# Every engine's instruction order as a table, with each tile's buffer named

## The chip, the cores and the metric

The kernel runs on one core of a Trainium2 chip. The metric is the device time of one execution in microseconds (us). The core has five engines with a queue each, which run side by side and meet at semaphores: PE (matrix multiply; PEld is its loading of weights), DVE and ACT (vector work and activation functions), POOL (a slower vector engine), and SP, which here issues the DMA transfers. An engine runs its own instructions strictly in the order in which the program lists them.

## The reference

Three layers follow each other, on a batch of 4, 576 tokens and 512 features (8 heads of 64):

```python
def attention(q, k, v):                       # (4, 8, 576, 64)
    pooled = repeat(softmax_attn(mean4(q), mean4(k), mean4(v)), 4)   # 144 pooled positions
    local = softmax_attn(q, k, v, mask=abs(i - j) < 4)
    return pooled + local                     # heads side by side: x, (4, 576, 512)

def moe(x):
    u = x + real(fft(fft(x, axis=1), axis=2))
    un = (u - mean(u)) / sqrt(var(u) + 1e-6)
    return u + maximum(un @ w_ch1, 0) @ w_ch2     # 512 -> 2048 -> 512

def moe2(x):
    gate = sigmoid(causal depthwise conv of 5 taps over the tokens)
    return (gate * (x @ w_val)) @ w_out
```

The result is float32. The weights arrive as float64 words.

## The kernel before

**Stages.** Each batch first goes through attention and the Fourier step: scores `dS` of the local band (a mask matmul from `bandb`, then products of kT and X), `exp` on ACT (dP), transposes (dPT, PT), values (dO); the pooled part `qkT`, `sc`, `E`, `eT`, `po`, `base`; then the FFT as matrix products (`ab`, AH and AL, then `pp`, `pq`, with the sum X<-X,DS). After it the batch is three units of 192 tokens, twelve in all. A unit has a layer normalization (`st`, `uc`, `sq`, `vv`, the root `r` by steps on POOL or DVE, and uh and ul, the f16 high and low part), eight h groups (`ph`, line 995) and eight c groups (`pc`, line 1015), each of 24 matmuls, since each product is made of three f16 passes (high x high, high x low, low x high). Between an h group and its c group ACT makes hh from ph and DVE the remainder hl. Then follow the sum X<-pc, and the third layer: yy (X in two f16 parts), the taps of the convolution, `val` (line 1107), gh and gl, `out` (line 1123), osb and its store. Unit (0,0) alone is computed in f32 (lines 957 and 970), because its weights aren't scaled yet.

**Weights.** They are loaded as words, put together on DVE in three integer steps (W<-W, W<-raw), and kept as f32 until a power of two to scale them by is known. For W1 ACT sums the squares (line 380), a PE product `tot` adds them across partitions, ACT makes f2s from it (line 259) and POOL turns it into s_w by p2a, p2b and s_w (lines 246, 248, 250). For W2 it is the product `gram` on PE, whose diagonal `tr<-gram,eye` DVE takes (line 179); gram lies in the bank that `pc` uses next. For w_val ACT squares (`sqw`), PE adds (`po<-sqw,corner`), DVE takes the maximum `cvmx`, and POOL makes s_wv. Then ACT writes the high part (line 406) and DVE the low one (line 176: W<-W,s_w,W).

**What sets the order.** All is written as small functions with a place in the program's order (`put`, `spread`; the P_ and S_ numbers), run in the order of their places. The framework then schedules each instruction by a time model and by priorities: `urgent` (line 184) raises a function's by the number of its kind in the table `U`. Loads are chained to each other (`load`, line 193). `behind` lets single instructions wait for an earlier one of another engine or the same, as the weights' conversion (line 300) for a step of the unit before. Batch 0's attention has a written order of steps, CHAIN0, which `line` holds engine by engine (line 344). Tiles of a ring (`bufs` of 2 or 3) take its buffers as they become free in the scheduled order. The loop at the end runs all of it:

```python
    for _, _, f in sorted(events):
        f()
```

Of the kernel before, what the change touches and what calls it, by code (L numbers as in the profile page):

```python
# [11 lines left out]
BF16 = mybir.dt.bfloat16  # L12
# [24 lines left out]
N_FILL = (8, 5, 14)  # L37
CHAIN0 = """
# [18 lines left out]
CHAIN = True  # L57
S_CH = 1.3
# [22 lines left out]
U = {'D': 4000, 'F': 3000, 'N': 3000, 'X': 600, 'M': 0, 'V': 1000, 'O': 0, 'W': 0, 'R': 2000, 'S': 4000}  # L81
# [55 lines left out]

@with_exitstack
def attn_moe_kernel(ctx, tc, q_t, k_t, v_p, v_w, w1, w2, w_val, conv_t, w_out, c_feat, c_seq, c_band, c_eye, c_plm, out):
# [4 lines left out]
    def pool(name, bufs=1, **kw):  # L144
        return ctx.enter_context(tc.tile_pool(name=name, bufs=bufs, **kw))
# [15 lines left out]
    dram = pool("dram", 2, space=bass.MemoryType.DRAM)  # L161
# [29 lines left out]
    chain = {"on": CHAIN, "last": None, "after": None}  # L191

    def load(**kw):

        if chain["on"] and chain["last"] is not None:
            with tc.issue_after(chain["last"]):
                i = nc.sync.dma_start(**kw)
        elif chain["after"] is not None:
            with tc.issue_after(chain["after"]):
                i = nc.sync.dma_start(**kw)  # L200
        else:
            i = nc.sync.dma_start(**kw)
        chain["last"] = i.ins

# [85 lines left out]
    gates, gates1, gates2 = [], [], []  # L290

    def behind(gate, f):

        if gate is None:
            f()
        else:
            with tc.issue_after(gate):
                f()

    def to_f32(dst, raw, gate=lambda: None):  # L300

        r = raw.rearrange("p (n t) -> p n t", t=2)
        behind(gate(), lambda: V.tensor_scalar(out=dst, in0=r[:, :, 1], scalar1=3, scalar2=0x3FFFFFF8,
                                               op0=ALU.logical_shift_left, op1=ALU.bitwise_and))
        behind(gate(), lambda: stt(V, dst, r[:, :, 1], -0x40000000, dst, ALU.bitwise_and, ALU.bitwise_or))
        last = []
        behind(gate(), lambda: last.append(stt(V, dst, r[:, :, 0], 29, dst, ALU.logical_shift_right, ALU.bitwise_or)))
        return last[0]

    def word_op(dst, raw, k):  # L310
# [5 lines left out]
        elif k == 1:  # L316
            stt(V, dst, r[:, :, 1], -0x40000000, dst, ALU.bitwise_and, ALU.bitwise_or)
        else:
            stt(V, dst, r[:, :, 0], 29, dst, ALU.logical_shift_right, ALU.bitwise_or)

# [21 lines left out]
    lined = {}  # L342

    def line(f):

        n0 = len(nc.cur_bb.bb.instructions)
        f()
        for i in nc.cur_bb.bb.instructions[n0:]:
            if i.engine != nc.sync.engine:
                if i.engine in lined:  # L350
                    tc.add_manual_dep(i, lined[i.engine], mybir.DependencyInfo(
                        mybir.DependencyClass.NoSync, mybir.DependencyReason.DATA), reason="line")
                lined[i.engine] = i.name

    def word_w(i):
        if i < 16:
            raw = raws.pop(i)
            n = 1024 // len(raw)
            pos = AT[i] if i < 8 else 8
            for z, x in enumerate(raw):  # L360
                last = to_f32(W[AT[i] + 1].bitcast(I32)[:, z * n:(z + 1) * n], x,
                       lambda g=gates if pos < 4 else gates1 if pos < 8 else gates2: g.pop(0) if len(g) > 1 else g[0])
            if i == 11:
                st[0]["worded"] = last
# [10 lines left out]
    def sumsq_w(i, key, first, last):  # L375

        if key == "w1":
            if first:
                gram[key] = keep.tile([P, 8], F32, name="ss_" + key)
            behind(st[0]["sq"].ins, lambda: A.activation(  # L380
# [478 lines left out]
    def ln(b, j):  # L859
# [27 lines left out]
        if head:  # L887
            st[0]["sq"] = i
# [825 lines left out]
```

## Time and profile before

| | us |
|---|---|
| median of 3 runs | 712.53 (712.43 to 714.36) |
| profiled execution, its own time | 715.93 |
| its span, first to last instruction | 714.1 |
| PE busy | 668.3 (94%) |
| DVE busy | 465.0 (65%) |
| ACT busy | 323.1 (45%) |
| POOL busy | 129.8 (18%) |
| mean granted clock of PE, as a share of 2.4 GHz | 0.974 |

Busy time is a sum over instructions, and the stages of the program differ: in the first 130 us weights arrive and batch 0 is prepared, then units follow each other, and the attention of the next batch runs between them. From some 520 us on only units are left. A stage is read from a table of windows: its length, the busy time of each engine in it, and the clock that PE was granted. The gap between length and busy time is the time the engine stood.

### The profile page before, as it was taken

What the parts mean: (1) busy time and instruction counts of PE and PEld (TensorE: products, weight loads), DVE (VectorE), ACT (ScalarE), POOL (GpSimd) and SP (SyncE); (2) the same over time, 40 slices, a digit from 0 to 9 for tenths busy, and PEclk for the clock granted to TensorE, in tenths of its full rate; (3) what the DMA queues carried; (4) which work ended last, traced back from release to release, by engine and by line L of the source; (5) the groups of instructions that cost most, each with busy time, mean ns of one, the idle gap of its engine ahead of it and who ended that gap; (6) DMA issues with size and microseconds to landing.
All of it is one profiled execution on the core that took longest, in us unless ns stands there. A gap on an engine that the chain in (4) does not pass through costs nothing. (4 is left out here: it accounts for less than half of the span.)

```text
span 714.1 us, 18255 instructions
## 1 busy us (share of the span) xinstructions
PE 668.3 (94%) x7778; PEld 588.7 (82%) x7779; DVE 465.0 (65%) x962; ACT 323.1 (45%) x985; POOL 129.8 (18%) x178
## 2 busy tenths in 40 slices
PE   7778998899989679999999999999999999999997
PEld 3555897889889568888898798798899989999895
DVE  4979999599884786548778527649435672723324
ACT  3843745693522556666334744744313232222212
POOL 0260042501121513230302324003100110000000
PEclk9968999999999879999999999999999999999999
DMA  9990144302333001330130001002000000000001
GB/s 331 410 339 2 59 178 161 122 31 81 127 113 115 17 1 40 112 104 16 60 110 1 25 25 35 17 35 79 4 17 16 2 17 16 2 17 2 30 2 45
DMA packets 23299, 52.08 MB, mean 73 GB/s; under 512 B 1855, under 2 KB 11071, under 8 KB 22194
## 3 DMA queue, kind: packets, MB, share of 16 engines
q1 hardware_dynamic: 23218, 50.91, 20.0%
q8 instruction: 61, 1.00, 0.6%
q14 instruction: 20, 0.16, 0.1%
HBM read 44.41 MB, written 8.26 MB: 74 GB/s over the span
## 5 line engine op out<-in xcount | busy, mean ns | idle before, releaser
L995 PE MATMUL ph<-uh,W 128*128 128x192 f16 x1408 | 195.4, 246 | 0.0
L995 PEld LDWEIGHTS <-W 128*128 128x128 f16 x2112 | 175.2, 98 | 5.9 <-issue 3.6
L995 PE MATMUL ph<-ul,W 128*128 128x192 f16 x704 | 173.2, 246 | 0.0
L1015 PE MATMUL pc<-hh,W 128*128 128x192 f16 x1232 | 170.8, 246 | 0.4 <-ACT hh L999 0.4
L1015 PEld LDWEIGHTS <-W 128*128 128x128 f16 x1848 | 153.3, 98 | 6.6 <-issue 4.5
L1015 PE MATMUL pc<-hl,W 128*128 128x192 f16 x616 | 150.4, 246 | 0.9 <-DVE hl L176 0.8
L176 DVE SCALAR_TENSOR_TENSOR hl<-ph,hh 128x384 f16<-128x384 f32 x88 | 48.5, 553 | 94.3 <-ACT hh L999 94.2
L999 ACT ACTIVATE hh<-ph 128x384 f16<-128x384 f32 x88 | 43.1, 490 | 101.1 <-PE ph L995 98.0
L1107 PE MATMUL val<-yy,W 128*128 128x192 f16 x576 | 55.7, 254 | 10.0 <-ACT yy L1049 6.6
L176 DVE SCALAR_TENSOR_TENSOR W<-X,cw,W 128x192 f32<-128x192 f32 x160 | 61.0, 435 | 0.7 <-ACT W L1070 0.5
L1107 PEld LDWEIGHTS <-W 128*128 128x128 f16 x576 | 50.5, 101 | 12.7 <-issue 6.5
L1123 PE MATMUL out<-W,gh 128*128 128x512 f16 x144 | 45.8, 379 | 0.0
L561 ACT ACTIVATE dP<-dS,dmx 128x64 f32<-128x64 f32 x120 | 36.0, 333 | 2.3 <-PE dPT L580 2.0
L179 POOL TENSOR_TENSOR E<-E,lsu 72x288 f32<-72x288 f32 x16 | 22.1, 1395 | 43.7 <-DVE lsu L694 22.8
L176 DVE SCALAR_TENSOR_TENSOR W<-W,W 128x1024 int32<-128x1024 int32 x24 | 29.2, 1237 | 0.1
L970 PE MATMUL pc<-h,W 128*128 128x192 f32 x128 | 24.9, 348 | 3.1 <-DVE tr L179 2.2
L1123 PE MATMUL out<-W,gl 128*128 128x512 f16 x72 | 27.3, 379 | 0.0
L561 ACT ACTIVATION_READ_ACCUMULATOR dP<-dS,dmx 128x1 f32 x120 | 27.2, 226 | 0.0
L176 DVE SCALAR_TENSOR_TENSOR X<-pc,iv,X 128x384 f32<-128x384 f32 x22 | 12.9, 613 | 20.0 <-PE pc L1015 20.0
L970 PEld LDWEIGHTS pc<-h,W 128*128 128x128 f32 x128 | 22.3, 202 | 3.8 <-DVE tr L179 2.4
L1123 PEld LDWEIGHTS <-gh 128*128 128x128 f16 x144 | 14.1, 98 | 13.6 <-issue 0.2
L182 POOL TENSOR_TENSOR sq<-sq 128x384 f32<-128x384 f32 (+1 forms) x12 | 11.9, 994 | 72.8 <-ACT sq L886 72.4
(287 smaller groups left out, 1228.6 us busy)
## 6 DMA issues: line engine op xcount, KB each, us to landing
W<-in_moe_w_ch_dram SPq DMA_DIRECT2D x12, 1024.0 KB
out_dram<-osb SPq DMA_DIRECT2D x17, 256.0 KB
vw<-in_vw_dram SPq DMA_DIRECT2D x8, 512.0 KB
X<-in_q_dram SPq DMA_DIRECT2D x6, 576.0 KB
v<-in_vp_dram SPq DMA_DIRECT2D x24, 144.0 KB
kT<-in_k_dram SPq DMA_DIRECT2D x4, 582.0 KB
X<-in_moe_w_ch_dram SPq DMA_DIRECT2D x2, 1024.0 KB
raw<-in_moe_w_ch_dram SPq DMA_DIRECT2D x4, 512.0 KB
```

Of the source, the lines that this page charges most:

```text
L176: return eng.scalar_tensor_tensor(out=out, in0=in0, scalar=scalar, in1=in1, op0=op0, op1=op1)
L179: return eng.tensor_tensor(out=out, in0=a, in1=b, op=ALU.mult)
L182: return eng.tensor_tensor(out=out, in0=a, in1=b, op=ALU.add)
L561: A.activation(out=s_[:, z, a], in_=pss[par][:, z, a], func=AF.Exp, scale=SCALE, bias=mx[:, par, z, a:a + 1], accum_out=su[:, par, z, a:a ...
L970: T.matmul(out=c["ps"][m // 2][:, m % 2], lhsT=W[9 + g][:, o:o + 128], rhs=hs[g // 2][:, g % 2, e, :], start=(kk == 0 and m % 2 == 0), sto ...
L995: T.matmul(out=ps[:, e], lhsT=w1_ap(pw, kc, 2 * g + e), rhs=uh[px][:, kc, :], start=(t == 0), stop=(t == 11))
L999: A.activation(out=h_, in_=ps, func=AF.Relu)
L1015: T.matmul(out=ps[m // 2][:, m % 2], lhsT=w2_ap(pw, kk, m), rhs=x[px][:, e, :], start=(kk == 0 and (pw, px) == (0, 0) and m % 2 == 0), sto ...
L1107: T.matmul(out=ps[:, e], lhsT=wv_ap(pw, kc, 2 * mh + e), rhs=m_["y"][px][:, kc, :], start=(t == 0), stop=(t == 11))
L1123: T.matmul(out=ps, lhsT=(gh, gl)[px][:, kc, t * 128:(t + 1) * 128], rhs=wo_ap(pw, kc), start=(n == 0), stop=(n == 11))
```

## The change

The numbers `U`, the priorities, the chains of loads, the gates `behind` and the helper `line` are gone. Two tables take their place. `ORDER` has one text for each engine, in which every instruction of the program stands once, as event and number within the event ("5.1" is instruction 1 of event 5, "0-3" a run of them). `SLOT` says for each tile of a ring which buffer it takes. Both were searched for offline; neither the search nor its model is in the source. Events are still made by `put` and `spread`, and what each instruction computes is the same. At the end each instruction is tied to the one ahead of it in its engine's text, without a semaphore, so that the scheduler can only list them in that order. PE, DVE, ACT, POOL and SP have the same instructions as before, one by one.

```diff
+SLOT = {
+    "ps_s.s": "010101010101010101010101010101010101010101010101010101010101011010010101010101010101010101010101010101010101010101010101010101010101010101001010101001010101010",
...
+ORDER = {
+    "sync": """
+4 0 1 2 7 3 6 9 11 5.1 5.0 10 8 13 14 15.0 12 15.3 15.1 15.4 198.1 15.5 15.2 125.0 198.0 124.1 16.2 124.0 121.0 16.1
...
-U = {'D': 4000, 'F': 3000, 'N': 3000, 'X': 600, 'M': 0, 'V': 1000, 'O': 0, 'W': 0, 'R': 2000, 'S': 4000}
...
+class Rings:
...
+    def tile(self, shape, dt, name, tag=None, bufs=None):
+        bufs = bufs or self.bufs
+        if tag is None or bufs == 1:
+            return self.pool.tile(shape, dt, name=name, **({"tag": tag} if tag else {}))
+        k = self.n[tag] = self.n.get(tag, -1) + 1
+        z = SLOT.get(f"{self.name}.{tag}")
+        return self.pool.tile(shape, dt, name=name, tag=f"{tag}_{int(z[k]) if z else k % bufs}")
...
-    def urgent(f, key):
-        if U[key]:
-            with tc.high_priority(offset=U[key]):
-                f()
-        else:
-            f()
...
     def load(**kw):
-
-        if chain["on"] and chain["last"] is not None:
-            with tc.issue_after(chain["last"]):
-                i = nc.sync.dma_start(**kw)
...
+        nc.sync.dma_start(**kw)
...
-    def behind(gate, f):
-
-        if gate is None:
-            f()
-        else:
-            with tc.issue_after(gate):
-                f()
...
-    put(S_G1[1], lambda: urgent(w1_scale, "S"))
+    put(S_G1[1], w1_scale)
...
+    engines = {n: getattr(nc, n).engine for n in ORDER}
+
+    def traced(f, n0):
+        f()
+        return [i for i in nc.cur_bb.bb.instructions[n0:] if "Boundary" not in type(i).__name__]
...
+    parts = [traced(lambda: None, 0)]
     for _, _, f in sorted(events):
-        f()
+        parts.append(traced(f, len(nc.cur_bb.bb.instructions)))
+    for name, eng in engines.items():
+        line = []
+        for x in ORDER[name].split():
+            n, _, r = x.partition(".")
+            ins = [i for i in parts[int(n)] if i.engine == eng]
+            z, _, y = r.partition("-")
+            line += ins[int(z):int(y or z) + 1] if r else ins
+        assert len(line) == len(set(i.name for i in line)) == sum(i.engine == eng for p in parts for i in p)
+        for x, y in zip(line, line[1:]):
+            tc.add_manual_dep(y, x.name, mybir.DependencyInfo(
+                mybir.DependencyClass.NoSync, mybir.DependencyReason.DATA), reason="order")
```

Three places of the order follow; the line numbers in rows of the new kernel are its own.

DVE, in the stage of the f32 unit, up to the diagonal `tr<-gram,eye` of W2. Before (W_115 and so on are weight tiles, s_w_1072 is W1's scale):

```order
L176 SCALAR_TENSOR_TENSOR W_115<-W_116,s_w_1072,W_115 128x1024
L176 SCALAR_TENSOR_TENSOR W_121<-W_123,W_121 128x1024
L564 TENSOR_SCALAR dsu<-dsu 128x16
L565 RECIPROCAL dsu<-dsu 128x16
L179 TENSOR_TENSOR dP_1254<-dP_1254,dsu 128x512
L179 TENSOR_TENSOR dP_1263<-dP_1263,dsu 128x512
L176 SCALAR_TENSOR_TENSOR W_116<-W_116,s_w_1072 128x1024
L176 SCALAR_TENSOR_TENSOR hl<-ph,hh 128x384
L179 TENSOR_TENSOR tr<-gram,eye 128x128
L395 TENSOR_REDUCE ss_w_1491<-tr 128x1
```

and with the change:

```order
L743 TENSOR_REDUCE dmx<-dS 128x8
L421 TENSOR_TENSOR dP_1254<-dP_1254,dsu 128x512
L421 TENSOR_TENSOR dP_1263<-dP_1263,dsu 128x512
L743 TENSOR_REDUCE dmx<-dS 128x8
L418 SCALAR_TENSOR_TENSOR W_121<-W_123,W_121 128x1024
L418 SCALAR_TENSOR_TENSOR W_115<-W_116,s_w_1072,W_115 128x1024
L421 TENSOR_TENSOR tr<-gram,eye 128x128
L584 TENSOR_REDUCE ss_w_1491<-tr 128x1
L418 SCALAR_TENSOR_TENSOR W_116<-W_116,s_w_1072 128x1024
```

The scaling of W_116 and the hl went behind the diagonal, and two maxima dmx came ahead of it.

POOL, around W1's scale s_w_1072 (ptv and vr are the pooled sums of v of batch 1, r the root of the layer normalization). Before:

```order
L246 TENSOR_SCALAR p2a<-f2s_w_1069 128x1
L248 TENSOR_SCALAR p2b<-p2a 128x1
L250 TENSOR_SCALAR s_w_1072<-p2b 128x1
L250 TENSOR_SCALAR iv_w_1073<-p2b 128x1
L901 TENSOR_SCALAR r_1167<-vv 128x192
```

and with the change:

```order
L424 TENSOR_TENSOR ptv<-v_1194 72x256
L424 TENSOR_TENSOR vr<-v_1195 72x256
L469 TENSOR_SCALAR p2a<-f2s_w_1069 128x1
L424 TENSOR_TENSOR ptv<-v_1365 72x256
L424 TENSOR_TENSOR vr<-v_1366 72x256
L424 TENSOR_TENSOR vr<-vr,ptv 72x256
L471 TENSOR_SCALAR p2b<-p2a 128x1
L473 TENSOR_SCALAR s_w_1072<-p2b 128x1
L424 TENSOR_TENSOR vr<-vr,ptv 72x256
```

The sums of v, which stood behind the root r, now stand ahead of the scale and between its steps.

POOL, around the scale of w_val (s_wv; f2s_wo leads to the scale of w_out). Before:

```order
L179 TENSOR_TENSOR dP_3048<-dP_3048,dsu 128x256
L182 TENSOR_TENSOR uc<-uc 128x192
L179 TENSOR_TENSOR r_2601<-r_2600 128x192
L246 TENSOR_SCALAR p2a<-cvmx 128x1
L179 TENSOR_TENSOR r_2601<-r_2601,vv 128x192
L248 TENSOR_SCALAR p2b<-p2a 128x1
L246 TENSOR_SCALAR p2a<-f2s_wo 128x1
L907 TENSOR_SCALAR r_2601<-r_2601 128x192
L250 TENSOR_SCALAR s_wv<-p2b 128x1
```

and with the change:

```order
L424 TENSOR_TENSOR X<-X,DS 128x287 x2
L667 MEMSET X 128x4x4
L469 TENSOR_SCALAR p2a<-cvmx 128x1
L471 TENSOR_SCALAR p2b<-p2a 128x1
L473 TENSOR_SCALAR s_wv<-p2b 128x1
L1084 TENSOR_SCALAR r_2600<-vv 128x192
L421 TENSOR_TENSOR r_2601<-r_2600 128x192
```

The three steps from cvmx to s_wv are together now, and r, dP and uc stand behind them.

## Rows read from the trace of the kernel before

**Rows 1.** The page's first part: busy time of each engine, share, instructions.

```profile
PE 668.3 (94%) x7778; PEld 588.7 (82%) x7779; DVE 465.0 (65%) x962; ACT 323.1 (45%) x985; POOL 129.8 (18%) x178
```

**Rows 2.** Windows: stretch, length, busy PE, PEld, DVE, ACT, POOL, clock, DMA share, GB/s.

```profile
0.00:78.00 78.00, 59.73 (x677) 39.62 (x678) 62.28 (x121) 38.33 (x163) 17.33 (x24) 0.87 0.66 248
78.00:130.10 52.10, 46.74 (x508) 44.00 (x508) 50.47 (x68) 30.67 (x90) 18.12 (x21) 1.00 0.40 144
130.10:240.00 109.90, 105.93 (x1208) 96.32 (x1208) 84.83 (x168) 55.30 (x166) 22.35 (x32) 0.98 0.27 92
240.00:260.00 20.00, 9.73 (x115) 7.95 (x115) 14.71 (x26) 15.36 (x46) 10.41 (x21) 0.66 0.05 16
260.00:520.00 260.00, 255.73 (x3169) 223.80 (x3168) 165.25 (x395) 134.62 (x431) 55.23 (x73) 1.00 0.14 47
520.00:714.10 194.10, 190.43 (x2110) 176.99 (x2108) 87.49 (x188) 48.81 (x93) 6.36 (x8) 1.00 0.04 14
```

**Rows 3.** Timeline of PE, 240 to 260: start, length, instruction, idle before and its releaser.

```profile
250.63 0.48 PE L1107 MATMUL val<-yy,W 128*128 128x192 f16 x2 [6.60 <-ACT yy L1049]
...
254.35 1.92 PE L1107 MATMUL val<-yy,W 128*128 128x192 f16 x11 [3.24 <-DVE yy L176]
```

**Rows 4.** Windows of the stretches at half clock: one of the four, and their sum.

```profile
246.40:260.00 13.60, 6.13 (x38) 5.56 (x39) 10.28 (x15) 11.64 (x32) 5.35 (x10) 0.50 0.00 1
sum 37.40, PE 27.36 PEld 22.16 DVE 28.85 ACT 23.18 POOL 17.63; mean PE 6.84 PEld 5.54 DVE 7.21 ACT 5.79 POOL 4.41
```

**Rows 5.** Timeline of DVE in the start.

```profile
9.32 1.35 DVE L1304 TENSOR_REDUCE qkT<-kTa 128x288 f32<-128x1152 f32 x1 [8.32 <-DMA kTa<-in_k_dram]
...
11.26 1.34 DVE L1304 TENSOR_REDUCE qkT<-X 128x288 f32<-128x1152 f32 x1
...
51.97 0.28 DVE L182 TENSOR_TENSOR X<-X,base 128x116 f32<-128x116 f32 x1 [4.51 <-ACT base L1354]
```

**Rows 6.** Timeline of DVE and PE around the diagonal of gram.

```profile
127.67 1.74 DVE L176 SCALAR_TENSOR_TENSOR W<-W,s_w 128x1024 f16<-128x1024 f32 x1
129.34 0.55 DVE L176 SCALAR_TENSOR_TENSOR hl<-ph,hh 128x384 f16<-128x384 f32 x1
...
129.80 0.28 DVE L179 TENSOR_TENSOR tr<-gram,eye 128x128 f32<-128x128 f32 x1
...
130.13 1.20 PE L970 MATMUL pc<-h,W 128*128 128x192 f32 x3 [2.23 <-DVE tr L179]
```

**Rows 7.** Timelines of DVE, POOL and ACT around the scale of w_val.

```profile
242.01 0.64 DVE L439 TENSOR_REDUCE cvmx<-po 128x1 f32<-128x512 f32 x1
243.08 0.69 DVE L555 TENSOR_REDUCE dmx<-dS 128x8 f32<-128x512 f32 x1 [0.42 <-PE dS L547]
...
248.27 1.56 DVE L176 SCALAR_TENSOR_TENSOR W<-W,s_wv,W 128x1024 f16<-128x1024 f32 x1
...
253.28 1.01 DVE L176 SCALAR_TENSOR_TENSOR yy<-X,s_y,yy 128x768 f16<-128x768 f32 x1
...
244.63 0.21 POOL L246 TENSOR_SCALAR p2a<-cvmx 128x1 f32<-128x1 f32 x1
...
246.46 0.19 POOL L250 TENSOR_SCALAR s_wv<-p2b 128x1 int32<-128x1 int32 x1
...
246.68 2.19 ACT L406 ACTIVATE W<-W,s_wv 128x1024 f16<-128x1024 f32 x2 [1.68 <-POOL s_wv L250]
...
249.64 0.93 ACT L1049 ACTIVATE yy<-X,s_y 128x768 f16<-128x768 f32 x1
```

**Rows 8.** Timelines of POOL and DVE, 93 to 123.

```profile
93.24 0.19 POOL L250 TENSOR_SCALAR s_w<-p2b 128x1 int32<-128x1 int32 x1
...
119.94 2.11 POOL L182 TENSOR_TENSOR ptv<-v 72x256 f32<-72x256 f32 x1 [17.94 <-DMA v<-in_vp_dram]
...
113.36 1.28 DVE L176 SCALAR_TENSOR_TENSOR W<-W,s_w,W 128x1024 f16<-128x1024 f32 x1
...
121.36 1.77 DVE L176 SCALAR_TENSOR_TENSOR W<-W,s_w,W 128x1024 f16<-128x1024 f32 x1
```

More of the change, by code (lines that the diff above doesn't have):

```diff
@@ L37 @@
 N_FILL = (8, 5, 14)
+SLOT = {
+    "ps_s.s": "010101010101010101010101010101010101010101010101010101010101011010010101010101010101010101010101010101010101010101010101010101010101010101001010101001010101010",
+    "ps_h.h": "0101011010101010101010101010101010101010101010101010101010101010101010101010101010101010101010101010101",
+    "ps_t.t": "010101010101101001010101101010101010100100101010101001010101001001010101010010101010010",
+    "startup.PT": "01001",
+    "mp.M": "01010010101010101",
+    "prp.E": "01201201201201202102120120120120120121021201201201220210210210210210210210120102102102100201201201201201201201210210210",
+    "tiny.p2a": "012012010210",
+    "tiny.p2b": "012012010210",
+    "m_tap.tap": "012012021021021020120102102012020121",
+    "m_L.L": "01001100110011001100110",
+    "tiny.r1": "011010101010",
+    "prp.pr": "0101010101010110101010010101",
+}
@@ L319, in word_op, with to_f32 @@
             stt(V, dst, r[:, :, 0], 29, dst, ALU.logical_shift_right, ALU.bitwise_or)
+    def to_f32(dst, raw):
+        for k in range(3):
+            word_op(dst, raw, k)
     raws = {}
@@ L358, in word_w @@
             n = 1024 // len(raw)
-            pos = AT[i] if i < 8 else 8
             for z, x in enumerate(raw):
[L361 to L364, printed above, removed]
+                to_f32(W[AT[i] + 1].bitcast(I32)[:, z * n:(z + 1) * n], x)
             return
@@ L379, in sumsq_w @@
                 gram[key] = keep.tile([P, 8], F32, name="ss_" + key)
-            behind(st[0]["sq"].ins, lambda: A.activation(
-                out=spare.bitcast(BF16)[:, 0:1024], in_=W[AT[i] + 1], func=AF.Square,
-                accum_out=gram[key][:, i % 8:i % 8 + 1]))
+            A.activation(out=spare.bitcast(BF16)[:, 0:1024], in_=W[AT[i] + 1], func=AF.Square,
+                         accum_out=gram[key][:, i % 8:i % 8 + 1])
             return
@@ L532, in scores @@
                 m = band[:, v0:v0 + n].unsqueeze(2).to_broadcast([P, n, 4, WK])
-                pss, bm = [], []
+                pss = []
                 for par in range(2):
                     ps = pst("dS", [P, n, 4, WK])
-                    behind(st[0]["ph"].ins if b == 1 and g == 0 else None, lambda: bm.append(T.matmul(
-                        out=ps, lhsT=eyeb, rhs=m, start=True, stop=False)))
+                    T.matmul(out=ps, lhsT=eyeb, rhs=m, start=True, stop=False)
                     pss.append(ps)
@@ L546, in scores @@
                                 row = slice(par * 64, par * 64 + 64)
-                                behind(bm[1].ins if z + a + hf + par == 0 else None, lambda: T.matmul(
+                                T.matmul(
                                     out=pss[par][hf * 64:hf * 64 + nq, z, a, 0:nk],
@@ L550, in scores @@
                                     rhs=kT[a // 2][row, a % 2, q0:q0 + nk],
-                                    start=False, stop=(z == n - 1 and a == 3)))
+                                    start=False, stop=(z == n - 1 and a == 3))
                 mx = tiny.tile([P, 2, n, 4], F32, tag="dmx", name="dmx")
@@ L607, in pool_qk @@
                 x = d["X"][:, 2 * z:2 * z + 2, PAD:PAD + S] if w == 0 else kT[z][:, :, HALO:HALO + S]
-                behind(st[0]["worded"].ins if b == 1 else None, lambda: V.tensor_reduce(
-                    out=d["qkT"][:, w, 2 * z:2 * z + 2], in_=x.rearrange("p a (g r) -> p a g r", r=4),
-                    axis=AX.X, op=ALU.add))
+                V.tensor_reduce(out=d["qkT"][:, w, 2 * z:2 * z + 2], in_=x.rearrange("p a (g r) -> p a g r", r=4),
+                                axis=AX.X, op=ALU.add)
             v1 = []
@@ L844, in attn_steps @@
         d["cuts"].append(n_chain)
-        steps[n_chain:] = [(c, lambda f=f: urgent(f, "F")) for c, f in steps[n_chain:]]
         return steps
@@ L868, in colsum @@
                 for c in range(4):
-                    behind(st[0]["ph"].ins if j else None, lambda c=c: st[b].update(st2=T.matmul(
-                        out=ps, lhsT=ones, rhs=src[:, c], start=(c == 0), stop=(c == 3))))
+                    T.matmul(out=ps, lhsT=ones, rhs=src[:, c], start=(c == 0), stop=(c == 3))
                 return ps
```

285 lines of the change are left out of this document (231 added, 54 removed), and 3 rows, old and new, of the table ORDER.

## The prediction, made before the changed kernel ran

> **What bounds the kernel now.** I read the busy times of the page first. PE works 94% of the span [rows 1], so the change can't win by work taken off PE: not one instruction is removed or added on any engine. What an order can win is time in which PE stands still, and time in which it runs at half its clock. The windows by stage show where that lies [rows 2]; the third number from a row's end is the granted clock as a share of 2.4 GHz. PE's idle time is the length of a stage less its busy time: 78.00 − 59.73 = 18.3 us in the start (attention of batch 0, weights arriving), 5.4 from 78 to 130.1 (the f32 unit), 4.0 to 240, 10.3 in the 20 us from 240 to 260, 4.3 from 260 to 520, 3.7 to the end, 45.8 in all. The two longest waits of PE both stand in the 20 us: 6.6 and 3.2 us in front of `val` [rows 3]. Then the half clock: four stretches at 0.50, that is 1.2 GHz, 37.4 us in all with PE busy for 27.36 of them [rows 4]. The last of them, from 246.4, sets in during the 6.6 us stand. Half of 27.36, 13.7 us, is what the lower level costs. So 45.8 + 13.7 = 59.5 us is the most that an order could give back, and a good part of it can't be: the first data must land, and each batch has one chain of scales that nothing else covers.
>
> **Part 1, the loads and the first stage (0 to 78 us).** DVE's first real instruction waits 8.32 us for the transposed k, at 9.32 us [rows 5]. In the new order DVE begins with the reduction of `X` (q) instead, and SP has loaded 562 KB less by then (1,374 against 1,936 KB, summed from the tile sizes in SP's order). At the 248 GB/s of the stage [rows 2] that is 2.3 us; but the first score now needs 1,146 KB instead of 798, 1.4 us more. PE's first waits are short and the pooled scores behind DVE are the longer chain, so I count −1.5 (0 to −2.3). DVE then stands 4.51 us at 51.97 for the pooled base of ACT [rows 5]. In the new order ACT runs base in two pieces between the transposes and DVE takes its sums in smaller lots. What is late next is the FFT fold behind them, so I take −3.5 of the 4.5 (0 to −4.5).
>
> **Part 2, the f32 unit (78 to 130.1).** Here DVE is busy for 50.47 of 52.10 us [rows 2], so an engine other than PE is the bound, and only what stands ahead of the instruction that PE waits for counts. That is `tr<-gram`, which empties the bank that `pc` needs: it starts at 129.80 and PE, after 2.23 us, at 130.13 [rows 6]. The new order takes from ahead of it a scaling of W (1.74), a hl (0.55) [rows 6] and a pooled reduction (1.34) [rows 5], and puts there two maxima of 0.69 each [rows 7]: 3.63 − 1.38 = 2.3 us less; five shorter steps go behind it too, and I count the row as 3 us shorter. PE meanwhile has 22 more of its own rows ahead of that `pc`, at some 46.74/508 = 0.09 us each [rows 2] 2 us of work that no longer comes later. I take −4 for the stage (0 to −5.4, its idle time). POOL now has v sums ahead of W1's scale: they lie on POOL, which waits for ACT then anyway, and cost nothing while their data is there (a rival below prices the other case). With part 1 that is **−9** to 130 us (−1 to −12).
>
> **Part 3, 130 to 240.** Idle 4.0 us, and a clock of 0.98, which is some 2 us more lost of 109.90 [rows 2]. Fewer conversions are left for DVE behind `tr`, and the covers between an instruction and its reader (the PE work queued between a transpose and its use, above all) are mostly longer in the new order. **−3** (0 to −6).
>
> **Part 4, the scale of w_val (240 to 260).** This is the clearest gain. The chain is: the maximum `cvmx` on DVE at 242.01 for 0.64; p2a on POOL only at 244.63, because POOL does two dP, one uc and an r first; p2b; s_wv at 246.46, again behind an r; ACT's two scalings from 246.68, in 2.19; yy at 249.64, behind three exps [rows 7]; `val` at 250.63 after 6.60 us, and again at 254.35 after 3.24, for the low halves [rows 3]. Of this POOL's part takes 246.65 − 244.63 = 2.0 us where its three steps have 0.6 us of work, and 2.0 more passed before it began. In the new order the three stand in a row, ahead of r, dP and uc; on ACT yy comes after one scaling, not two; and the squares on PE that feed `cvmx` come 57 `pc` matmuls before `val` (earlier nearly none lay between): 57 x 0.09 = 5.1 us, with the score products 7. The chain from the end of PE's squares to yy, as it was, takes some 8.6 us (242.0 to 250.6); less 4.0 − 0.6 on POOL and half of 2.19 on ACT it is 4.1, so it fits beneath the 7. What remains is the low half: scaling 1.56 and yy 1.01 on DVE [rows 7] against 11 `val` and 3 `pc` at 0.09, 1.3 us, so 1 to 3 us of waiting stay. PE's work in the window is 9.73 us, of which 6.13 was at half clock [rows 2, 4]: at the full level 6.7. 20 − 6.7 − 2.3 = **−11** (−6, where only POOL's delay goes and the lower level stays, to −13).
>
> **Part 5, 260 to the end.** Idle 4.3 and 3.7 us in 454 us [rows 2]. Small waits of under a microsecond; from 260 to 520 the longer covers take **−3** (0 to −4). In the tail the order before is in whole blocks of 24 matmuls, and it is cut up afterwards with some covers shorter (the reuse of a `pc` bank from 3.3 us of PE work to 1.8): **+1** (−1 to +4).
>
> The sum is −9 − 3 − 11 − 3 + 1 = **−25 us**. The profiled execution took 715.93 us with a span of 714.1, so it comes to 691 on that footing; against the median of 712.53, which the profiled one lies 3.4 above, it is **687.5**.
>
> **A rule against the change.** While POOL summed v, from 119.94 on, the scaling `W<-W,s_w,W` on DVE took 1.77 us (121.36); with POOL idle at 113.36 it took 1.28 [rows 8]. The Trainium skill ("SBUF — State Buffer", Who interferes with whom) says that a DVE instruction with two SBUF inputs contends with a GpSimd instruction that reads SBUF; the trace agrees, with 0.49 us. By that rule, six v sums moved up into the DVE-bound stretch would each hold DVE up, 6 x 0.49 = 2.9 us, and the time would be 690; by the rows alone they only change their place within the bound stretch, where they stood at its end before, and the sum stays. It is inside the range.
>
> **The rivals.** *Deeper* (below 676): the three other half-clock stretches go as well. They hold 27.36 − 6.13 = 21.2 us of PE's busy time [rows 4], so up to 10.6 us more, 677, and with parts 1 to 3 at their better ends 667. For it: each lies near a gap that gets shorter. Against: DVE's and the loads' limits there remain.
>
> *Partial* (699 to 710): the gaps are exchanged. Every engine's order is now fixed to the last instruction, so a duration other than the search assumed makes the engine stand where before something else was equally bound to wait. There are 88 groups of hidden activations, each with a hand-off from PE through ACT and DVE to PE; 0.15 us at each is 13 us, 687.5 + 13 = 700.5. Against it: the order before was a fixed order on each engine too, and waits little after 260 [rows 2].
>
> *Slower*: the v sums block W1's scale. Ahead of s_w on POOL now stand five sums of v. In the trace before, W1's scale is done at 93.24 + 0.19 and the v sums first begin at 119.94, after 17.94 us of waiting for their data, with 2.11 us for the first [rows 8]. If the loads land no earlier than before, five sums at 2.11 us or half of it bring s_w to 125 to 130, 32 to 37 us late, and behind it stand ACT's eight scalings and DVE's, then all of unit (0,1). PE's f32 work covers some 5 of it; 687.5 + 30 = 717.5. It decides from about 25 us of net delay, which is v landing after some 114 us. Against it: in the new order of SP the loads for these sums stand ahead of the second round of raw weights, no longer behind the third and vw, and p2a itself comes earlier, since ACT takes all of W1's squares before the first `sq`.
>
> *No change* (within 0.3%, about what a measurement of this kernel can tell from none, 710.4 to 714.7): the stages are bound by transfers. The window from 240 speaks against it, with a DMA share of 0.05 [rows 2].
>
> **How the numbers follow.** My forecast of 676 to 699 has a chance of 0.62: its largest part, the scale of w_val, is read off a chain whose detours are plainly gone, and the others can miss by half. Deeper 0.14, partial 0.11, no change 0.04, slower 0.09. Faster by over 0.3% is 0.62 + 0.14 + 0.11 = 0.87, same 0.04, slower 0.09. The range is 667 to 704: it takes in nearly all of the deeper case (0.12, to the end that was worked out) and half of the partial one (0.06), and leaves out the two last: 0.80.
>
> **What would show it.** In the profile after: PE's waits in front of the first `val` of batch 0 under 3 us together, with a granted clock of 1.00 around it; s_wv within 2 us of `cvmx`; `tr<-gram` some 8 to 9 us earlier than 129.80; W1's scale before 93; PE's idle time near 25 us. I am wrong if PE shows new waits beyond 260 of more than 8 us in all, if the first v sum still begins near 120, or if half-clock stretches come up behind new gaps.

## The result and the profile after

The changed kernel takes **673.44 us** (median of 4, 673.12 to 674.41) against 713.33 (712.43 to 714.36, 4 runs beside it): a ratio of 0.944, 95% interval 0.942 to 0.946, 39.9 us less. That is inside the stated range of 667 to 704, 14 us below the forecast of 687.5, and a little below the 676 to 699 that the main forecast covered. The profiled execution has a span of 671.6 us (714.1 before) and a mean granted clock of 0.981 (0.974).

The page's busy line of the new kernel, which answers [rows 1]:

```profile
PE 649.7 (97%) x7778; PEld 580.4 (86%) x7779; DVE 459.2 (68%) x962; ACT 321.3 (48%) x985; POOL 126.6 (19%) x178
```

PE stands 21.9 us now, not 45.8. But its busy time has fallen too, from 668.3 to 649.7 us, with the same 7778 matmul records. The lower clock accounts for some 3.5 of these 18.6 us (below). The other 15 come from something that the prediction didn't think of.

For the comparison by stage the cuts of [rows 2] are no use as they stand, since the same work now comes earlier. I gave each kind of PE instruction its usual spacing at full clock, added these up along the kernel before to 78, 130.1, 240, 260 and 520 us, and cut the new kernel where the same sum is reached. The windows (length first, then busy time of PE, PEld, DVE, ACT and POOL, the granted clock, DMA share, GB/s):

```profile
0.00:73.29 73.29, 61.48 (x677) 41.83 (x677) 60.40 (x118) 44.88 (x176) 11.93 (x24) 0.84 0.75 263
73.29:122.38 49.09, 46.52 (x505) 43.99 (x506) 48.09 (x64) 22.58 (x80) 17.36 (x21) 1.00 0.42 139
122.38:220.13 97.75, 97.19 (x1205) 91.42 (x1205) 87.95 (x179) 58.72 (x172) 23.40 (x36) 1.00 0.30 102
220.13:227.06 6.93, 6.21 (x124) 5.54 (x121) 4.51 (x7) 5.49 (x7) 5.85 (x8) 1.00 0.02 4
227.06:477.38 250.32, 247.74 (x3184) 221.70 (x3183) 167.62 (x393) 139.75 (x457) 57.17 (x76) 1.00 0.15 47
477.38:671.60 194.22, 190.54 (x2095) 175.88 (x2093) 90.68 (x205) 49.89 (x96) 10.87 (x13) 1.00 0.07 21
```

Against the lengths in [rows 2]:

| stage (cuts of before) | before, us | after, us | difference | foretold |
|---|---|---|---|---|
| start, 0 to 78 | 78.00 | 73.29 | −4.7 | −5 |
| f32 unit, to 130.1 | 52.10 | 49.09 | −3.0 | −4 |
| to 240 | 109.90 | 97.75 | −12.2 | −3 |
| scale of w_val, to 260 | 20.00 | 6.93 | −13.1 | −11 |
| to 520 | 260.00 | 250.32 | −9.7 | −3 |
| tail | 194.10 | 194.22 | +0.1 | +1 |

So four terms hold and two are far too small. In the third and fifth stage PE hardly stood before (4.0 and 4.3 us of idle time), and it stands 0.6 and 2.6 us now. Of the 21.8 us that they gave together, 5.1 were idle time, and the rest was hidden in PE's busy time.

**The scale of w_val.** The timelines after, of DVE, POOL, ACT and PE (start, length, instruction, in brackets the idle time before and its releaser), answer [rows 3, 7]:

```profile
216.40 0.68 DVE L628 TENSOR_REDUCE cvmx<-po 128x1 f32<-128x512 f32 x1
217.17 0.21 POOL L469 TENSOR_SCALAR p2a<-cvmx 128x1 f32<-128x1 f32 x1 [10.46 <-DVE cvmx L628]
217.74 0.19 POOL L473 TENSOR_SCALAR s_wv<-p2b 128x1 int32<-128x1 int32 x1
221.35 0.94 ACT L1230 ACTIVATE yy<-X,s_y 128x768 f16<-128x768 f32 x1
222.78 0.26 PE L1288 MATMUL val<-yy,W 128*128 128x192 f16 x1
223.76 0.41 PE L1288 MATMUL val<-yy,W 128*128 128x192 f16 x3 [0.72 <-DVE yy L418]
```

s_wv follows `cvmx` by 1.3 us (4.5 before), yy begins 1.4 us before `val`, and one wait of 0.72 us stays of 9.84.

**PE's busy time.** The same work keeps PE busy for less time. Windows from 130 to 520 us of the products `sc` alone, before and after (PE's busy time, then PEld, DVE, ACT):

```profile
130.00:520.00 390.00, 13.57 (x96) 8.18 (x96) 10.49 (x24) 20.44 (x96) 0.98 0.17 58
130.00:520.00 390.00, 8.59 (x96) 5.44 (x96) 9.95 (x24) 20.47 (x96) 1.00 0.18 60
```

and of the products `po<-ET,vr`, by their line (PE, PEld):

```profile
130.00:520.00 390.00, 13.97 (x96) 7.53 (x96) 0.98 0.17 58
130.00:520.00 390.00, 8.53 (x96) 5.32 (x96) 1.00 0.18 60
```

These are 96 records each and 5.0 and 5.4 us less. Such sums show where to look, but they are no price, since a record's length overlaps its neighbours': `eT`, whose blocks have no fixed cost (last section), falls from 12.18 to 8.18 us by the same sum as its groups are put together. The reason is seen where they stand among f16 matmuls. Before, one `po` product (two records, since it is f32), later the other three; after, all four, and four of `sc` at once:

```profile
154.56 0.33 PE L1015 MATMUL pc<-hh,W 128*128 128x192 f16 x2
155.19 0.46 PE L721 MATMUL po<-ET,vr 72*64 72x144 f32 x2 [0.31 <-ACT ET L716]
155.80 0.24 PE L1015 MATMUL pc<-hl,W 128*128 128x192 f16 x1
```

```profile
148.21 0.71 PE L908 MATMUL po<-ET,vr 72*64 72x144 f32 x8
148.85 0.71 PE L863 MATMUL sc<-qkT 64*72 64x144 f32 x8
149.49 0.26 PE L1176 MATMUL ph<-uh,W 128*128 128x192 f16 x1
```

These products use half of the PE array: a `sc` has 64 rows (`par * 64` in its code), a `po` fills 64 columns. I took the price of a block as the time from the start of the last f16 product ahead of it to that of the first behind, less the 0.08 us that an f16 product takes anyway, where no wait is in it. It is 0.48 us with one `po`, 0.73 with three, 0.74 with four; 0.73 with two `sc` of the same half and 0.74 with four. The halves run side by side when both stand together, and a block with half of them takes as long as a whole one. A second product of the same half adds 0.25 us (0.48 to 0.73), so about 0.24 us of each block don't depend on what is in it. The Trainium skill ("TensorEngine Tiling (Array Packing)", Key Properties) says that a change of the array's tiling mode drains TensorE, and that different tiles work in parallel. The traces agree with both, if these products among full ones are such a change: 0.24 us at each block, and four products in the time of two. A drain as such isn't seen in a trace. Before, 19 of the 24 `sc` and `po` groups of batches 1 to 3 are split up by f16 matmuls (seven of `sc`, twelve of `po`); after, none. Each split is one block more, so at the prices above they cost 7 × 0.73 + 12 × 0.48 = 10.9 us. The values `dO` (64 rows by 64 columns) are cut up before too, and went from 10.93 to 9.24 us by the sum of their records.

**The lower clock.** It has gone only in part where the deeper rival put it. Of the four stretches of [rows 4] the one at 130 us (3.4 us long) and the one around the scale of w_val are gone. The two in the start, 3.4 and 17.1 us long, have become one of 23.9; its window:

```profile
32.32:56.20 23.88, 20.33 (x205) 15.36 (x203) 20.42 (x45) 11.03 (x35) 6.55 (x5) 0.50 0.99 326
```

PE is busy there for 20.33 us, against 27.36 in all four stretches before: at half of it, some 3.5 us back, no more.

### The profile page after: what moved, and what is told of

Its sections match the earlier page's. It is cut to its first block, busy times and chain, and to the rows that moved or that the text cites. A ratio compares the mean times of both kernels' runs of the same rounds, so it can differ in the third digit from the quotient of the medians.

```text
span 671.6 us, 18209 instructions
## 1 busy us (share of the span) xinstructions
PE 649.7 (97%) x7778; PEld 580.4 (86%) x7779; DVE 459.2 (68%) x962; ACT 321.3 (48%) x985; POOL 126.6 (19%) x178
## 4 chain that ended last, share of the span: by engine, by line
PE 78%; DVE 10%; POOL 2%; ACT 1%; issue 0%; ACTq 0%; POOLq 0%; DVEq 0%
PE ph L1176 25%; PE pc L1196 24%; PE out L1304 7%; PE val L1288 7%; DVE W L418 3%; PE pc L1151 2%; PE ab L976 2%; PE po L908 1%; PE st L1060 1%; PE dO L785 1%; PE sc L863 1%; PE pp L999 1%; PE pq L999 1%; PE eT L898 1%; PE dPT L768 1%; POOL r L421 1%
## 5 line engine op out<-in xcount | busy, mean ns | idle before, releaser
L1176 PE MATMUL ph<-uh,W 128*128 128x192 f16 x1408 | 198.0, 246 | 0.3 <-ACT uh L1104 0.3
L1196 PE MATMUL pc<-hl,W 128*128 128x192 f16 x616 | 134.0, 246 | 0.5 <-DVE hl L418 0.5
L418 DVE SCALAR_TENSOR_TENSOR W<-X,cw,W 128x192 f32<-128x192 f32 x160 | 63.7, 438 | 9.8 <-ACT W L1251 9.3
L1288 PE MATMUL val<-yy,W 128*128 128x192 f16 x576 | 58.9, 246 | 0.7 <-DVE yy L418 0.7
L421 POOL TENSOR_TENSOR E<-E,lsu 72x288 f32<-72x288 f32 x16 | 18.1, 1144 | 67.2 <-DVE lsu L1515 34.0
L1196 PE MATMUL pc<-hh,Wz 128*128 128x192 f16 x176 | 25.6, 246 | 0.0
L1140 PE MATMUL ph<-u,W 128*128 128x192 f32 x128 | 23.0, 329 | 1.0 <-DVE u L1690 1.0
```

Of the source, the lines that this page charges most:

```text
L418: return eng.scalar_tensor_tensor(out=out, in0=in0, scalar=scalar, in1=in1, op0=op0, op1=op1)
L421: return eng.tensor_tensor(out=out, in0=a, in1=b, op=ALU.mult)
L1140: T.matmul(out=ps[:, e], lhsT=W[AT[kc * 2 + m // 8] + 1][:, o:o + 128], rhs=u()[:, kc, :], start=(kc == 0), stop=(kc == 3))
L1176: T.matmul(out=ps[:, e], lhsT=w1_ap(pw, kc, 2 * g + e), rhs=uh[px][:, kc, :], start=(t == 0), stop=(t == 11))
L1196: T.matmul(out=ps[m // 2][:, m % 2], lhsT=w2_ap(pw, kk, m), rhs=x[px][:, e, :], start=(kk == 0 and (pw, px) == (0, 0) and m % 2 == 0), sto ...
L1288: T.matmul(out=ps[:, e], lhsT=wv_ap(pw, kc, 2 * mh + e), rhs=m_["y"][px][:, kc, :], start=(t == 0), stop=(t == 11))
```

## The experiments

`SLOT` holds exactly the buffers that the allocator gave the tiles before. With before's order written into `ORDER`, the program of before comes out instruction by instruction. All runs below have the `SLOT` of the new kernel, and those with nearly all of before's order (the sixth has three of POOL's instructions moved, nothing else) take before's time. So all of the gain is order, and orders of the two can be mixed. Each run has the kernel before beside it (715.7 to 716.7 us there), and its ratio is to that. PE's losses are the times from the start of one record to the start of the next, as far as they exceed the usual ones of their kind: "short" losses are those under 250 ns, longer ones are called stands.

**1 and 2. The new order up to a point, then the old one.** The first takes the new order for the first 73 us (118 of DVE's 962 instructions, 449 of PE's 6805; most f32 products are one instruction and leave two of the 7778 records), the second until just ahead of the first `val` (360 and 1833).

```diff
 each engine's text in ORDER:
-the order before
+the new order up to its last instruction begun before 73.2 us (second run: 222.2)
+then all others, in the order before
```

> The first 73 us of the new order (all that each engine had started there by 73.2 us, just ahead of the first f32 product ph<-u), then everything else in the order of before. Buffers are those of both kernels. Theory (the gain adds up by stages, and this stage is worth 4.6 us): 708 us. Rival (a gain in the start is given back, since DVE binds the next stage): 711 to 714, no change.

> The new order for all that each engine had started by 222.2 us (just ahead of the first val), then the order of before for the rest. Theory (stages add up): 27 to 28 us are gained before val, nothing is given back, and what the new order gains behind it, some 12 us, is missing: 685 us. Rival (the old rest gives part of it back in new waits, since other engines' work is left over in another state): 692 to 700.

Measured: 714.86 us, ratio 0.999 (0.998 to 1.001), and 693.76, 0.970 (0.968 to 0.972). The first 73 us alone bring nothing. DVE starts u 5 us earlier, and `tr` comes 0.4 us earlier (129.80 before), as these rows of its DVE timeline show:

```profile
71.78 0.95 DVE L1613 TENSOR_TENSOR u<-X,st 128x768 f32<-128x768 f32 x1 [0.33 <-PE st L1609]
75.95 0.18 DVE L440 TENSOR_SCALAR cw<-craw 128x20 int32<-128x20 int32 x1 [2.85 <-DMA craw<-in_moe_conv_w_dram]
88.57 0.69 DVE L440 TENSOR_SCALAR W<-W 128x1024 int32<-128x1024 int32 x1 [1.80 <-DMA W<-in_moe_w_ch_dram]
129.40 0.28 DVE L344 TENSOR_TENSOR tr<-gram,eye 128x128 f32<-128x128 f32 x1
```

DVE sets the end of the next stage, and being ready earlier it waits longer for loads in the order of before: 4.7 us in the two waits shown, where the kernel before waits 1.5 for loads up to `tr`. The rival was right. The second run gains 22.1 us on the kernel beside it, where 27 to 28 were foretold. At the first `val` it has them (223.19 against the 250.63 of [rows 3], 27.4 us), and it gives some of them back in one place, the next low half, where PE stands 8.89 us against 3.24 before. Its PE timeline at the joint:

```profile
223.19 0.34 PE L1224 MATMUL val<-yy,W 128*128 128x192 f16 x2
232.43 1.44 PE L1224 MATMUL val<-yy,W 128*128 128x192 f16 x8 [8.89 <-DVE yy L354]
```

s_wv was there at 217.64, but DVE, by the old order, first does dmx, ivvo (which waits for POOL) and uc, and makes the low half of yy only behind them. So a scale that is ready early is worth little unless ACT's, DVE's and PE's orders go along: this run's stage of w_val gains 2.7 of the 13.1 us.

**3, 4 and 5. The half-array products.** Into the order before: the 19 split groups put together (3), or the 12 of them that are `po` alone (5). Into the new order: all 24 groups split by eight f16 matmuls (4). PE's order alone is touched. The third and fifth do this, at one place (between the rows shown lie f16 products of a c group and of the next h groups):

```diff
-MATMUL po<-ET,vr 64x144
 MATMUL pc_1992<-hl,W_117 128x192
...
-MATMUL po<-ET,vr 64x144 x3
+MATMUL po<-ET,vr 64x144 x4
```

> The order of before, with one edit on PE: in the pooled attention of batches 1 to 3 the four sc products and the four po products of a step stand together at the place of the last of them (19 of 24 groups were split by f16 matmuls). Theory (each block of f32 products between f16 matmuls costs a fixed time, some 0.73 us for two sc as for four, 0.48 us for a single po): 7 x 0.73 + 12 x 0.48 = 10.9 us less, 702 us. Rival (what counts is only the waits; small spacings are no cost of the blocks): 711 to 714, or slower, since the first products of a group now come up to 7 us later.

> The new order, with one edit on PE: each of the 24 groups of sc and po in batches 1 to 3 is split in two by eight f16 matmuls (two sc and two, one po and three). Theory (a fixed time for each block): 12 x 0.73 + 12 x 0.48 = 14.6 us more, 688 us. Rival (only waits count): 673 to 675.

> The order of before with one edit on PE: only the twelve po groups of batches 1 to 3 stand together at the place of their last product; their reader needs all four anyway, so no step waits longer for its input. Theory (a half-width product that runs alone between f16 matmuls costs 0.48 us, in its group nothing): 12 x 0.48 = 5.8 us less, 707. Rival (as in the run with sc gathered too, the gain goes into new waits): 711 to 715.

Measured: together 717.06 (1.001, 0.999 to 1.004); split 702.89 against 673.44 unsplit, 29 us more; `po` alone together 712.10 (0.994, 0.992 to 0.996). Windows of `sc` in the split run, and of `po` (by its line) in the split one and in the one with `po` together:

```profile
130.00:520.00 390.00, 18.29 (x96) 11.48 (x96) 10.15 (x24) 20.57 (x96) 0.98 0.18 60
130.00:520.00 390.00, 13.97 (x96) 7.53 (x96) 0.98 0.18 60
130.00:520.00 390.00, 8.70 (x96) 5.48 (x96) 0.98 0.18 58
```

The price of a split block is shown in both directions: `po` takes 13.97 us split and 8.5 to 8.7 together, whichever kernel it is in, and by their spacing the blocks of the fourth run cost 0.73 (two `sc`), 0.73 (three `po`) and 0.48 us (one) too. (Part of the 18.29 of `sc` is half clock.) The short losses rise by 15.2 us where the new order is split (14.6 foretold) and fall by 9.5 where the old one is gathered (10.9 foretold), 5.0 with `po` alone (5.8).

What the whole gathering gained, though, came back as stands, since an early product now waits at the last one's place and a late one holds up what reads it. New ones among the waits of PE in the gathered run (engine, line waited for; sum, times, longest):

```profile
PE eT L810 <- POOL E L333: 3.3, 1, 3.3
PE sc L775 <- ACT dP L661: 3.1, 1, 3.1
```

and in the split run, which it made slower by more than the blocks cost:

```profile
PE ph L1179 <- DVE hl L421: 4.6, 2, 4.0
```

Stands above 250 ns grew by 9.1 us where `sc` and `po` were gathered, and by 9.8 where they were split, and the lower clock cost 2.7 and 3.6 us more; for the split run 15.2 + 9.8 + 3.6 = 28.6 us is the whole loss. (How this sum divides depends on how records at half clock are counted: kept apart, they make it 11.2 + 11.6 + 5.8.) With `po` alone the new stands cost 1.4 us, and 3.6 us of gain stay. So the shape of the blocks is one cause, and it has to be bought in an order that doesn't pay for it elsewhere.

**6, 7 and 8. The chain of w_val's scale, in the order before.** First POOL's three steps alone, put ahead of the dP and uc. Then DVE and ACT as well (yy after one scaling, the exps behind). Then also PE's squares, 37 `pc` earlier. The first and the ACT part of the second:

```diff
 TENSOR_SCALAR r_2600<-vv 128x192
+TENSOR_SCALAR p2a<-cvmx 128x1
+TENSOR_SCALAR p2b<-p2a 128x1
+TENSOR_SCALAR s_wv<-p2b 128x1
 TENSOR_TENSOR dP_3043<-dP_3043,dsu 128x256
 TENSOR_TENSOR dP_3048<-dP_3048,dsu 128x256
 TENSOR_TENSOR uc<-uc 128x192
 ...
-ACTIVATE dmx<-dmx 128x16
-ACTIVATE W_121<-W_122,s_wv 128x1024 x2
-ACTIVATE dP_3181,dsu<-dS,dmx 128x64 x3
+ACTIVATE W_121<-W_122,s_wv 128x1024
 ACTIVATE yy<-X,s_y_2713 128x768
```

> The order of before with one edit on POOL: the three steps from cvmx to s_wv stand together, ahead of the two dP, the uc and the rest of r (s_wv some 3 us earlier, 243.6 for 246.5). By the prediction's own step (what POOL's detour costs goes, the lower clock stays: 6 of 11 us): 707 to 709 against 713. Rival, after the second run (first222, in which s_wv was there early and PE still stood 9 us before the low halves of val): the low half of yy on DVE stands behind ivvo, which waits for POOL's iv_wo, and behind uc, which waits for r; val's first two products come 3 us earlier, the others at the same time: 712 to 715, no change.

> As the run before, and the other two engines of the chain: on DVE the steps to s_y ahead of cvmx, and the two low scalings and the low half of yy ahead of iv_y and ivvo; on ACT one scaling, yy, the other scaling, ahead of the next maxima and exps. PE as before. Theory: val starts at 246 for 250.6, its low halves at 247.6 for 254.35, 6.7 us less, and more where the half-clock stretch goes: 702 to 706. Rival (w_out's scale and uc, which now come later, hold out or the next unit up): 709 or more.

> As the run before, and PE's four products of the squares 37 pc matmuls earlier, ahead of the variance st, with cvmx on DVE, the POOL steps and the first scaling on ACT at the front of their engines as well. Theory: s_wv at 241, yy at 244.4 behind ACT's squares for w_out; val at 245.3 and 246.4, that is 8 us less, and the lower clock goes: 700 to 704. Rival (cover on PE was not what bound it): as the run before.

Measured: 716.29 (1.001, 0.999 to 1.002), 714.57 (0.998, 0.997 to 1.000), 714.54 (0.999, 0.997 to 1.000). The first moves s_wv from 246.46 to 244.39 and gains nothing. PE's waits before `val` in it (before: 6.60 and 3.24):

```profile
249.92 0.47 PE L1201 MATMUL val<-yy,W 128*128 128x192 f16 x2 [4.81 <-ACT yy L1143]
255.81 0.48 PE L1201 MATMUL val<-yy,W 128*128 128x192 f16 x2 [5.42 <-DVE yy L331]
```

The second takes these waits down to 1.96 and 1.46 us, and the stretch at half clock from 13.6 to 6.8 us (245.1 to 251.9). Another 3.4 us at half clock come up at 258.8, behind a stand at the next hand-off, the low half of u for the unit that follows:

```profile
245.09 0.48 PE L1201 MATMUL val<-yy,W 128*128 128x192 f16 x2 [1.96 <-ACT yy L1143]
247.03 1.28 PE L1201 MATMUL val<-yy,W 128*128 128x192 f16 x7 [1.46 <-DVE yy L331]
257.19 0.24 PE L1089 MATMUL ph<-ul,W 128*128 128x192 f16 x1 [2.15 <-DVE ul L1018]
```

The DVE work that was put back (iv_y, ivvo, uc) stands on the path of ul. By the cuts used above the stage of w_val's scale takes 20.3 us in the first run and 13.4 in the second and third, in place of 20.00. But most of these 6.6 us go at once: from what PE does at 235 us of the kernel before to what it does at 264, the three runs are 0.3 us longer, 0.7 and 2.4 us shorter. In the third, s_wv comes some 3 us earlier than in the second, measured from the same work of PE, but on ACT two squares for w_out stand ahead of yy (it begins at 248.46, 5.5 us behind s_wv).

**9. The passes of PE in another sequence, in the new kernel.** The waits that stay in it are for low halves, each with products of the high half behind it. The edit stands in `val`, in `out` and in the first two h groups of a unit.

```diff
-for kc in range(4):
-    for pw, px in PASS:
+LATE = [(kc, p) for kc in range(4) for p in ((0, 0), (1, 0))] + [(kc, (0, 1)) for kc in range(4)]
+for kc, (pw, px) in LATE:
```

> The new kernel, with the passes inside an accumulation of PE written in another sequence: in val, in out and in the first two h groups of a unit (not of unit (0,1)) the eight products with the high half (uh, yy high, gh) come first and the four with the low half (ul, yy low, gl) last; the places in the order stay. Theory (PE's 97% are the bound here, so a stand of PE that is filled with its own later work is gained for good): of the waits for low halves at 222.8 to 236.4, 0.7 for yy, 0.9 for ul, 0.5 and 0.7 for gl, nearly all go, about 2.5 us with what the restart costs, 671 (669.5 to 672). Rival (the stand moves to the next hand-off, as in the single edits of the kernel before): within 0.5 us of 673.4.

Measured: 673.61 us (673.11 to 674.01), the new kernel's 673.44 again, and a span of 671.3 against 671.6. The waits for yy and ul are gone, and these are there:

```profile
224.82 0.67 PE L1288 MATMUL val<-yy,W 128*128 128x192 f16 x6 [1.33 <-DVE W L418]
236.29 0.60 PE L1303 MATMUL out<-W,gl 128*128 128x512 f16 x2 [1.13 <-DVE gl L418]
```

`val` now wants the low half of w_val earlier than DVE has it, and both waits for gl have become one. DVE's row of results sets the pace there, and PE's own order no longer helps. The rival was right.

**10 and 11. The new order from a point on, and in one stretch alone.** The tenth run is the order before up to 205 us, then the new one. The eleventh returns to the order before after the first `out` tiles (651 of PE's instructions, 83 of DVE's, 62 of ACT's and 32 of POOL's are in new order).

```diff
 each engine's text in ORDER:
 the order before, up to its last instruction begun before 205 us
-the rest in the order before
+the rest in the new order (eleventh run: what it begins before 246.5 us, then again the order before)
```

> Up to 205 us of the kernel before its order on every engine, the new order for all that is left: the complement of the run with the new order in the first part, with the joint ahead of the squares of w_val. Theory (each stage keeps its own gain where all engines follow the new order in it): the stage of w_val gives 10, 200 to 260 of PE's work 4.5, 260 to 380 7 and the end 1, so 715.5 - 22.5 = 693 (690 to 698). Rival (the second part gains only because the first part brought weights, scales and scores forward, so that the new order finds them early): 703 or more.

> The new order in one stretch alone, on every engine: up to 205 us of the kernel before its order, then the new one until shortly after the first out tiles (651 of PE's 6805 instructions, 83 of DVE's, 62 of ACT's, 32 of POOL's), then the rest in the order of before. Theory (what the three engines' single edits didn't bring, since the next hand-off took it back, comes when all five orders of that stretch are changed together): the stage of w_val gives 10 and the 17 us ahead of it 3, so 715.5 - 13 = 702.5 (699 to 707). Rival (what a stretch gains is given back where the old order begins again, as after the first 73 us): 710 or more.

Measured: 691.13 (0.965, 0.962 to 0.969), as the theory had it; and 710.0 (0.991, 0.989 to 0.993), 6.7 us less than the kernel beside it, at the edge of the rival's 710 and short of the theory's 699 to 707. With the same cuts by PE's work, the windows of w_val's stage in the two runs, and the one behind it in the eleventh:

```profile
236.80:244.04 7.24, 6.38 (x123) 5.51 (x121) 5.00 (x8) 5.62 (x9) 5.73 (x8) 1.00 0.02 4
238.90:246.06 7.16, 6.30 (x123) 5.43 (x121) 5.16 (x8) 5.51 (x8) 5.52 (x7) 1.00 0.01 2
246.06:514.16 268.10, 256.87 (x3169) 223.74 (x3168) 175.37 (x409) 141.32 (x459) 61.09 (x81) 1.00 0.15 48
```

In both the stage takes 7.2 us in place of 20.00. It needs nothing that the first 205 us of the new order bring. But where the old order begins again, the stage to 520 takes 268.10 us, 8.1 more than before. Of this 5.0 are four stands of PE at the joint:

```profile
266.10 0.38 PE L644 MATMUL dS<-bandb 128*128 128x512 bf16 x1 [0.94 <-ACT dP L668]
268.14 0.38 PE L644 MATMUL dS<-bandb 128*128 128x512 bf16 x1 [1.09 <-ACT dP L668]
271.37 0.57 PE L1207 MATMUL val<-yy,W 128*128 128x192 f16 x5 [1.59 <-ACT X L710]
277.33 0.59 PE L979 MATMUL st<-sq,ones 128*128 128x192 f32 x2 [1.40 <-POOL sq L343]
```

Read from these releasers, the new order had put ACT's and POOL's work for the next attention and unit behind w_val's, and the order after it has covers for that, which the old order lacks; no run tests this by itself. The second and tenth run together gain 46.8 us, more than the whole (39.9): both have the new order from 205 to 222 us, the second has 2.7 us of w_val's stage too, and stages in the order of before came out 1 to 3 us longer or shorter from run to run. Finer than that their sum isn't a measure.

## Why the prediction held, and where it didn't

**Start and f32 unit, −9.** Measured −7.7, 4.7 and 3.0, and `tr` came at 123.71, 6.1 us earlier where I had 8 to 9. The working held: DVE's first reduction begins at 8.10 us in place of 9.32, its wait for the pooled base is 0.46 us in place of 4.51, and PE no longer waits for `tr`. What it didn't say is that the two terms are not to be had apart: with the start alone in new order the gain was gone at `tr`.

**130 to 240, −3, and 260 to 520, −3.** Measured −12.2 and −9.7, outside the bounds I gave for them. The step that failed is the premise in the first paragraph, that the change can't win by work taken off PE, since no instruction goes. I counted idle time and half clock, with 59.5 us as the most that there is, and took busy time as given. But the time that a product takes depends on what stands beside it: the 19 split groups of `sc` and `po` cost 10.9 us more than whole ones, by the price of their blocks. The Trainium skill's sentence on the drain, which I didn't weigh, points there. The trace of before alone showed it too: at 142.16 us four records of `sc` take 0.71 us, and at 148.86 eight take 0.71 as well.

**Scale of w_val, −11.** Measured −13.1, and the signs that I named came: s_wv 1.3 us behind `cvmx`, 0.72 us of waiting before `val`, a clock of 1.00. The chain was the right one, but its reading as a sum of detours was too simple. POOL's 2 us were worth nothing alone. The detours of three engines were worth 6.6 us in the stage and 0.7 behind the next hand-off, with PE's squares 6.6 and 2.4. The whole stretch in new order was worth 12.8, of which the old order behind it took back 8.1. That the place of the wait moves to the next low half (yy, then W, then ul) is what the single edits show.

**Tail, +1.** Measured +0.1, inside its bounds.

**The rivals.** *Deeper*: the time fell below 676, so the size was the rival's, but not the mechanism. Half clock gave back some 3.5 of the 13.7 us that it cost; what the forecast lacked came from the blocks and from stands in the third and fifth stage. So it is partly luck that 673 lies in the range: its lower end was there for the clock. That end is also added up wrongly, since parts 1 to 3 at their better ends take 677 to 671 and not to 667; and the least of parts 1 and 2 together is 0, not −1. *Partial*, gaps exchanged: not in the changed kernel, where PE's idle time is 21.9 us (I had said near 25) and its waits beyond 260 are small. But it is just what happened in the third, sixth and eleventh run. *Slower*: W1's scale didn't wait for v. POOL's rows show the first sum of v long before the 119.94 of [rows 8], and the scale 9.5 us earlier:

```profile
70.99 0.81 POOL L424 TENSOR_TENSOR ptv<-v 72x256 f32<-72x256 f32 x1 [5.62 <-ACT Wz L570]
83.77 0.19 POOL L473 TENSOR_SCALAR s_w<-p2b 128x1 int32<-128x1 int32 x1
92.23 2.24 POOL L424 TENSOR_TENSOR ptv<-v 72x256 f32<-72x256 f32 x1 [7.58 <-DMA v<-in_vp_dram]
```

Only sums behind s_w wait for a load (7.58 us here, 9.24 at 113.66), and no wait of PE, DVE or ACT there is put down to them. The three sums between p2a and p2b (79.98 to 83.52) weren't free, though, as part 2 has it: ACT waits 2.4 us for s_w behind them.

**The rule.** The Trainium skill ("SBUF — State Buffer", Who interferes with whom) has a DVE instruction with two SBUF inputs contend with a GpSimd instruction that reads SBUF, and the trace after agrees. Of DVE and POOL in the f32 unit:

```profile
102.18 1.64 DVE L418 SCALAR_TENSOR_TENSOR W<-W,s_w 128x1024 f16<-128x1024 f32 x1
102.70 1.72 POOL L424 TENSOR_TENSOR ptv<-v 72x256 f32<-72x256 f32 x1
124.90 1.28 DVE L418 SCALAR_TENSOR_TENSOR W<-W,s_w 128x1024 f16<-128x1024 f32 x1 [0.58 <-ACT W L595]
```

Beside the sum of v the same scaling takes 1.64 us, alone 1.28. But only two of the six scalings from 87 to 126 us meet one (the other takes 1.75), so it is 0.8 us and not the 2.9 that six would have cost; the stage came out 1 us longer than I forecast.

What stays open: the 21.8 us of the two stages can't be split to the microsecond. PE's idle time has 5.1 of them, the stretch of 3.4 us at half clock from 130.3, in which PE was busy throughout, 1.7, and the blocks 10.9 by their price; the 4 that are left aren't assigned. The fourth run prices the blocks at 15 us, with more splits than the order before had. And which of the remaining 21.9 us of PE's idle time another order could still take isn't known; one try at 3 us of it gave none.

## What to carry to other kernels

Read busy time as something that can shrink: where a bound engine runs small products that fill half of its array, count their blocks between other work, and put the two halves together. Price an order by stretches, with all engines in it, and look at the first hand-off behind the stretch, for that is where most of the partial edits here gave their gain back. An edit on one engine that gains nothing doesn't show that the place is worth nothing: POOL's edit alone gained nothing, and those of three and four engines 0.7 and 2.4 us behind the next hand-off, in a stage from which all orders together took 12.8.

## What was not expected of the hardware

A block of half-array f32 products among f16 matmuls took 0.48 us with one product, 0.73 with two of one half, and 0.74 with all four of both halves; two such groups behind each other 1.38 (at 148.21), so only the halves run together and not the groups. `eT` transposes, f32 too but 72 by 72 and so not in a half, had no such extra: 0.19 us for three, 0.31 for five, 0.50 for eight. Nor had `st`, an f32 product on the whole array: 0.35 us alone among f16 matmuls, where two such records within a row of them (`pc<-h`) take 2 × 0.16. So it isn't the f32 that costs it. And the lower clock came up at stands that edits made, not only where loads are late: in the split kernel PE ran at 0.50 from 141.2 to 151.5 us, which sets in during a stand of 4.0 us in front of `ph` (139.3 to 143.25), where the new order unsplit has 1.00 throughout.
